# Gated mix of attention and a gated MLP: first loads on two queues, single last stores, and the last 512 rows of x turned by the load

## Chip, cores and metric

One core of one Trainium2 chip. The metric is the device time of one execution in microseconds (us). Before the change, three runs took 268.17, 269.15 and 270.21 us, median 269.15.

## What is computed

x has 2048 rows of 512 elements, bf16. Two branches start from it and are mixed row by row by a gate:

```python
x = A_x
g = _sigmoid((x * gate_w).sum(-1, keepdims=True))
# a: 32 query heads of 16, one key and one value head for all of them
q = (x @ wq) in heads;  k = x @ wk;  v = x @ wv
a = softmax(q k^T * 16**-0.5) v @ wo
# b: spatial gating MLP
z = gelu(x @ w_in)                    # 1376 = 2 * 688 columns
z1, z2 = z[..., :688], layernorm(z[..., 688:])
b = (z1 * (w_sp @ z2 + b_sp[:, None])) @ w_out
return g * a + (1 - g) * b
```

The kernel doesn't form the 2048x2048 scores. It replaces exp by a polynomial of third degree, so that the sums over all keys become moments of k and v that are computed once; a guard at the end checks that the scores were small enough, and a general path stands by if not.

## The kernel before, in words

**A planner writes the order.** The kernel describes its work as tasks (`Plan.add`, line 327), each with an engine or a choice of two, an estimated cost, what it reads and writes, and a priority (lower goes first). `Plan.run` (line 380) simulates the five engines and the DMA pipe with those estimates and so fixes each engine's program order; on the chip every engine then runs its program strictly in that order and waits on semaphores. `TUNE` (line 65) changes priority and earliest time of single tasks by their number, 25 of them before the change. DMAs of SP are issued in SP's planned order, those of ACT in ACT's. Free PSUM banks are given out by the planner too (`allowed`, line 1311); a group of products (`Group`) holds its bank until its copy out of PSUM.

**Start.** VectorE fills a tile with zeros, and TensorE runs `WARM` = 9 products of 128x512 on it (lines 843 and 844), which compute nothing. `ld_x(c)` (line 846) loads 512 rows of x, 512 KB, as they lie in memory. SP issues x's first chunk, the identity matrix `ident`, the two halves of w_in's second part (`win2`, line 851), x's second chunk, `wq` (line 857), x's third and fourth chunk, and the constants cf, cs and th (lines 860 to 862; th goes into a part of the buffer Pr). ACT issues wk, wv and gate_w (`gwl`, lines 852 to 855), then loads its table for Gelu.

**x is turned.** Nearly all products need x with its columns on the partitions (`xT`). `g_x(c)` (line 877) does this for a chunk by 16 products of 128x128 with `ident`, four to a PSUM bank, and copies the four banks to xT on ACT or VectorE (line 884). The untouched x lies in `xn`, which is the first half of the buffer of w_sp's rows (wT, line 744), so the first loads of w_sp wait for x to be read.

**After that, per chunk:** `g_kv(c)` computes k, v and the gate's sum (line 887; the copies and features follow on VectorE and POOL), `moments(c)` sums the features (line 938), and `moments_out()` makes the small matrices of the polynomial (line 948). Beside it TensorE computes the second part of z (`g_z2`, line 1121; 16 tiles, two halves, four products each) and the first two of 16 units of queries (`g_q`, line 1008; a unit is four heads for 512 rows).

**Queries go through DRAM.** The queries of a unit are stored to `qe` (line 1019) and come back spread over the partitions as Y and in part as X (`y_load`, line 1024). The load of w_in's first part (`win1`, line 1253) and the loads of w_sp are held until the first Y loads are planned. `g_z1` (line 1151) needs win1. w_sp is loaded by transposing DMAs, 128 rows to an issue, 512 KB (`ld_wT`, line 1162), each waiting for the one before; these are the only transposing loads before the change.

**Units and output.** `unit(u)` (line 1054) multiplies the third-degree form by Y: product (line 1074), then either VectorE alone (line 1083) or ACT and POOL (lines 1087, 1088). `g_sp` (line 1172) is the product with w_sp, `g_out` (line 1208) the last product, its scaling and its store. In the last 512 rows the stores go two tiles at a time, 256 KB (line 1226). Before the first of these SP waits for all other DMAs and reads the guard's flag (`finish`, line 1452).

In the profile, line 774 is the helper that records most products of 128x128 at the start, 779 and 808 those that use a part of the array; so tiles, not lines, tell these apart.

Of the kernel before, what the change touches and what calls it, by code (L numbers as in the profile page):

```python
# [34 lines left out]
WARM = 9  # L35
# [29 lines left out]
TUNE = {40: (-3, 0), 330: (0, 700), 383: (-25, 0), 403: (-3, 0), 435: (-25, 1500), 500: (-3, 0), 519: (-6, 300),  # L65
# [597 lines left out]
def build_kernel(nc, x_d, wq_d, wk_d, wv_d, wo_d, win_d, wsp_d, bsp_d, wout_d, gw_d, out_d):  # L663
    es = ExitStack()
    with es:
# [180 lines left out]
        def ld_x(c):  # L846
            load("sp", lambda q: q.dma_start(xn[:, 4 * c:4 * c + 4, :], x2[512 * c:512 * c + 512, :].rearrange("(k p) n -> p k n", p=128)), [("xn", c)], size=524288, pri=c, tag="x")
        ld_x(0)
        load("sp", lambda q: q.dma_start(ident[:], id_d), ["id"], size=32768, pri=0)
        for h in range(2):  # L850
            load("sp", lambda q, h=h: q.dma_start(win[:, :, FH + 344 * h:FH + 344 * h + 344], win_d[:, FH + 344 * h:FH + 344 * h + 344].rearrange("(dt p) n -> p dt n", p=128)), [("win2", h)], size=352256, pri=0)
# [3 lines left out]
        load("act", lambda q: q.dma_start(gwl[:], gw_d.rearrange("(one n) -> one n", one=1)), ["gwl"], size=1024, pri=-3)  # L855
        ld_x(1)
        load("sp", lambda q: q.dma_start(wq[:], wq_d.rearrange("(dt p) n -> p dt n", p=128)), ["wq"], size=524288, pri=1.5)
# [19 lines left out]
        def g_x(c):  # L877

            for dt in range(4):
                g = Group("any")  # L880
                for k in range(4):
                    add("pe", 60.0, mm1(lambda g=g: g.b, 128, 128 * k, xn[:, 4 * c + k, 128 * dt:128 * dt + 128], ident[:], True, True), r=["id", ("xn", c)], grp=g, pri=-1, tag="xT")
# [279 lines left out]
        def ld_wT(tc):  # L1162
            load("sp", lambda q: [q.dma_start(bspz[64 * i:64 * i + 1, tc % 2, :], bsp_d[512 * tc:512 * tc + 512].rearrange("(one t) -> one t", one=1)) for i in range(2)], [("bspz", tc % 2)], size=4096, n=2, pri=13, chan="bsp%d" % (tc % 2), hold=[yld[0]] if tc < 2 else [])
            for k in range(4):
                r0 = 512 * tc + 128 * k
                load("sp", lambda q, r0=r0, k=k: q.dma_start_transpose(wT[:, tc % 2, :, 128 * k:128 * k + 128], wsp_d[r0:r0 + 128, :]),
                     [("wT", tc % 2, k)] + (kfeat if tc == 1 else [("xn", c) for c in range(4)] if tc == 0 else []), size=524288, rate=DMA_TR, pri=13, chan="wT%d_%d" % (tc % 2, k), tag="wT", after=([wtl[0]] if wtl[0] else []), hold=([yld[0]] if tc < 2 else []))
                wtl[0] = pl.tasks[-1]
# [39 lines left out]
        def g_out(t2):  # L1208
# [27 lines left out]
        for c in range(4):  # L1236
            g_x(c)
# [311 lines left out]
```

## Time and profile before

| what | us |
|---|---|
| median of three runs | 269.15 |
| the profiled execution, own time | 269.58 |
| its span, first to last instruction | 267.8 |
| around the span | 1.8 |
| PE busy | 256.4 |
| DVE busy | 176.2 |
| POOL busy | 174.5 |
| ACT busy | 161.3 |

The span is what the profile's views cover; the time of a run is 1.8 us longer. PE is TensorE, PEld its weight loads (they lie beside products), DVE VectorE, POOL GpSimd, SP the engine that issues most DMAs. A matmul's length in the views contains its way through the array, so products that follow each other overlap; their spacing is the cost of one.

### The profile page before, as it was taken

To read this page: it belongs to the slowest core of one execution; us is meant where nothing else is said; L and a number is where in the kernel's file an instruction comes from. 1 tells how busy PE (TensorE), PEld (TensorE's weight loads), DVE (VectorE), ACT (ScalarE), POOL (GpSimd) and SP (SyncE) were. 2 spreads that over 40 slices of the span, in tenths; PEclk is the share of its full clock that TensorE was granted. 3 is DMA by queue.
4 is the path that set the end of the run, shared out by engine and by line. 5 is a ranking of instruction groups with operands and counts; after the bars stand their busy time and mean duration, and the time that the engine had idled before them with its cause. 6 is when DMAs were issued, how large, how long until landed. Compare 5 with 4: busy or idle time off the path is not lost. (4 is left out here: it accounts for less than half of the span.)

```text
span 267.8 us, 8031 instructions
## 1 busy us (share of the span) xinstructions
PE 256.4 (96%) x3378; PEld 124.0 (46%) x3379; DVE 176.2 (66%) x312; ACT 161.3 (60%) x209; POOL 174.5 (65%) x105
## 2 busy tenths in 40 slices
PE   7999979999999999989999989999999999999992
PEld 3686758863444433424444334434444434344450
DVE  1797969367686575784777575667687576679320
ACT  2685857789754769886476747382656563652203
POOL 8693111134697489758888989695786999998000
PEclk9999999999999999999999999999999999999998
DMA  7949975501666689969999996649697670523112
GB/s 186 350 173 245 225 93 129 81 16 53 162 214 179 143 206 184 173 175 144 217 197 222 206 251 156 189 116 226 167 184 203 147 181 14 145 85 96 39 44 84
DMA packets 54186, 42.18 MB, mean 158 GB/s; under 512 B 36249, under 2 KB 47746, under 8 KB 54146
## 3 DMA queue, kind: packets, MB, share of 16 engines
q1 hardware_dynamic: 53088, 41.59, 67.0%
q8 instruction: 27, 0.44, 0.7%
q10 hardware_dynamic: 1058, 0.03, 0.2%
q14 instruction: 13, 0.11, 0.2%
HBM read 28.51 MB, written 4.72 MB: 124 GB/s over the span
## 5 line engine op out<-in xcount | busy, mean ns | idle before, releaser
L1088 POOL TENSOR_TENSOR Pr<-Wt,Y 128x1024 bf16<-128x1024 bf16 x64 | 136.2, 2128 | 45.2 <-ACT Wt L1087 35.8
L1087 ACT ACTIVATE Wt<-ps,T1c 128x1024 bf16<-128x1024 f32 x64 | 71.3, 1114 | 53.3 <-PE ps L1074 31.7
L1083 DVE SCALAR_TENSOR_TENSOR Pr<-ps,T1c,Y 128x1024 bf16<-128x1024 f32 x64 | 81.1, 1278 | 27.1 <-PE ps L1074 26.9
L808 PE MATMUL ps<-wT,z 64*128 64x512 bf16 x598 | 92.0, 376 | 0.0
L1074 PE MATMUL ps<-X,T 64*128 64x512 bf16 x256 | 46.9, 379 | 2.1 <-ACT Wt L1087 1.2
L808 PEld LDWEIGHTS ps<-wT,z 64*128 64x128 bf16 x598 | 34.0, 94 | 31.2 <-issue 1.5
L1045 ACT ACTIVATE X<-ps 128x1024 bf16<-128x1024 f32 x32 | 31.7, 1022 | 5.5 <-PE ps L1042 5.5
L808 PE MATMUL ps<-wout,z 64*128 64x512 bf16 x169 | 30.5, 376 | 0.0
L1074 PEld LDWEIGHTS ps<-X,T 64*128 64x128 bf16 x256 | 12.0, 93 | 26.0 <-ACT Wt L1087 8.3
L808 PE MATMUL ps<-wo,win 64*128 64x512 bf16 x112 | 21.9, 377 | 0.0
L1127 ACT ACTIVATE z<-ps 128x344 bf16<-128x344 f32 x32 | 14.3, 459 | 10.0 <-PE ps L774 5.8
L779 PE MATMUL ps<-Pr,cs 128*32 128x512 bf16 x256 | 19.5, 381 | 0.0
L1192 DVE TENSOR_TENSOR z<-ps,z 128x512 bf16<-128x512 f32 x20 | 13.7, 685 | 8.2 <-PE ps L808 8.2
L1134 POOL TENSOR_TENSOR rstd<-ve,nhalf 128x4 f32<-128x4 f32 x4 | 4.3, 1080 | 20.6 <-DVE ve L1133 20.6
L1220 ACT ACTIVATE outsb<-ps,G 128x512 bf16<-128x512 f32 x10 | 6.8, 687 | 17.5 <-PE ps L808 17.1
L1116 POOL TENSOR_TENSOR win<-Ns,Rb 128x512 bf16<-128x512 f32 x12 | 15.3, 1272 | 2.4 <-POOL Pr L1088 0.7
L1129 DVE BATCH_NORM_STATS2 bst<-z 128x6 f32<-128x344 bf16 x32 | 14.5, 491 | 2.6 <-ACT z L1127 2.6
L808 PEld LDWEIGHTS ps<-wout,z 64*128 64x128 bf16 x169 | 11.1, 94 | 9.5 <-issue 0.2
L1097 DVE SCALAR_TENSOR_TENSOR Prd<-ps,T1d,Qt 128x512 bf16<-128x512 f32 x16 | 11.9, 746 | 4.3 <-PE ps L779 4.1
L779 PE MATMUL ps<-xT,win 128*32 128x512 bf16 x260 | 14.7, 379 | 0.0
L1158 ACT ACTIVATE z<-ps 128x512 bf16<-128x512 f32 x20 | 11.7, 596 | 2.9 <-PE ps L779 2.9
L774 PE MATMUL ps<-win,xT 128*128 128x344 bf16 x68 | 12.7, 309 | 0.4 <-DMA win<-in_B_w_in_dram 0.4
(148 smaller groups left out, 335.6 us busy)
## 6 DMA issues: line engine op xcount, KB each, us to landing
Y<-qe SPq DMA_DIRECT2D x32, 512.0 KB, 5.5
Rb<-rd SPq DMA_DIRECT2D x14, 256.0 KB, 5.3
wT<-in_A_x_dram SPq DMA_DIRECT2D x4, 512.0 KB, 7.9
qe<-Qt SPq DMA_DIRECT2D x64, 32.0 KB
out_dram<-outsb SPq DMA_DIRECT2D x12, 128.0 KB, 2.9
X<-qe SPq DMA_DIRECT2D x32, 32.0 KB
Pr<-c_third SPq DMA_DIRECT2D x1, 784.0 KB, 9.0
win<-in_B_w_in_dram SPq DMA_DIRECT2D x2, 344.0 KB, 5.5
```

The source lines that it names most:

```text
L774: return lambda t: t.matmul(bank(b(), n, off), lhsT, rhs, start=start, stop=stop)
L779: return [t.matmul(ps[32 * q:32 * q + 32, 512 * b() + off:512 * b() + off + n], lhsTs[q], rhss[q], start=start, stop=stop, tile_position=( ...
L808: return lambda t: t.matmul(bank(b(), n, off), lhsT[h], rhs[h], start=start, stop=stop, tile_position=(64 * z, 0))
L1045: add("act", 1030.0, lambda a, g=g, v=v: a.activation(X[:, ub, v:v + 3:2, :], bank(g.b, 1024).rearrange("p (j n) -> p j n", j=2), ACT.Square),
L1074: return [p.matmul(bank(gw.b + e), T3[64 * e:64 * e + 64, t, :], X[64 * e:64 * e + 64, ub, j, :], start=True, stop=True, tile_position=(64 ...
L1083: add("dve", 1290.0, lambda v, wv=wv, pi=pi, yv=yv, t=t: v.scalar_tensor_tensor(Pr[:, pi, :, :], wv(), T1c[:, t:t + 1], yv, ALU.add, ALU.m ...
L1087: add("act", 1040.0, lambda a, wv=wv, wi=wi, t=t: a.activation(Wt[:, wi, :, :], wv(), ACT.Identity, bias=T1c[:, t:t + 1]), r=["T1c"], w=[( ...
L1088: add("pool", 2130.0, lambda v, wi=wi, pi=pi, yv=yv: v.tensor_tensor(Pr[:, pi, :, :], Wt[:, wi, :, :], yv, ALU.mult), r=[("Y", yb, h), ("W ...
L1116: ot = lambda v, u=u, G=G: v.tensor_tensor(OT[:, tg % 2, G, :], Ns[:, u % NNS, :], rbt(G), ALU.mult)
L1127: add("act", 456.0, lambda a, g=g, h=h: a.activation(z2[:, FH * st + 344 * h:FH * st + 344 * h + 344], bank(g.b, 344), ACT.Gelu_apprx_tanh ...
L1129: add("dve", 495.0, lambda v, h=h: v.bn_stats(bst[:, st, h, :], z2[:, FH * st + 344 * h:FH * st + 344 * h + 344]), r=[("z2", st, h)], w=[( ...
L1192: add("dve", 690.0, lambda v: v.tensor_tensor(dst, bank(g.b), dst, ALU.mult), w=[("z1", ft, tc)], grp=g, evac=True, pri=3.5, tag="u")
```

## The change

- The warm-up has 7 products in place of 9.
- The first chunk of x is loaded in two halves of 256 KB. `ident`, the first half of win2 and gwl are issued by ACT, in this order and ahead of wk and wv. The second half of win2 stays on SP.
- `g_x` turns the first two 128-row tiles of a chunk for all four column blocks, then the other two, so that its four banks are open at once.
- wq's priority goes from 1.5 to 5, which places it behind x's third chunk and the new loads.
- The last 512 rows of x are not loaded to xn and not turned by products: four transposing loads of 128 rows, 128 KB each, write xT (one semaphore count for all four). They have priority 4.5 on SP's queue. `g_x(3)` is gone with its 16 products and four copies. w_sp's first loads wait only for the other three chunks.
- The last two tiles of the output are stored singly, 128 KB each; the two before them stay a pair.
- TUNE is another table, with 18 entries; task numbers have shifted.

```diff
-WARM = 9
+WARM = 7
...
-TUNE = {40: (-3, 0), 330: (0, 700), 383: (-25, 0), 403: (-3, 0), 435: (-25, 1500), 500: (-3, 0), 519: (-6, 300),
...
+TUNE = {39: (0, 1500), 316: (-12, 0), 434: (-1, 3000), 487: (-25, 0), 500: (-12, 0), 553: (6, 0), 668: (-12, 1500),
...
-        def ld_x(c):
-            load("sp", lambda q: q.dma_start(xn[:, 4 * c:4 * c + 4, :], ...), [("xn", c)], size=524288, pri=c, tag="x")
-        ld_x(0)
-        load("sp", lambda q: q.dma_start(ident[:], id_d), ["id"], size=32768, pri=0)
-        for h in range(2):
-            load("sp", ... win[:, :, FH + 344 * h:FH + 344 * h + 344] ..., [("win2", h)], size=352256, pri=0)
+        def ld_x(c, parts=1):
+            n = 4 // parts
+            for h in range(parts):
+                load("sp", lambda q, h=h: q.dma_start(xn[:, 4 * c + n * h:4 * c + n * h + n, :], ...),
+                     [("xn", c, k) for k in range(n * h, n * h + n)], size=131072 * n, pri=c, tag="x")
...
+        load("act", lambda q: q.dma_start(ident[:], id_d), ["id"], size=32768, pri=-3)
+        ld_x(0, 2)
+        ld_win2("act", 0, -3)
+        ld_win2("sp", 1, 0)
+        load("act", lambda q: q.dma_start(gwl[:], gw_d.rearrange("(one n) -> one n", one=1)), ["gwl"], size=1024, pri=-3)
...
         ld_x(1)
-        load("sp", lambda q: q.dma_start(wq[:], ...), ["wq"], size=524288, pri=1.5)
-        for c in range(2, 4):
-            ld_x(c)
+        load("sp", lambda q: q.dma_start(wq[:], ...), ["wq"], size=524288, pri=5)
+        ld_x(2)
...
+        load("sp", lambda q: [q.dma_start_transpose(xT[:, :, 1536 + 128 * k:1664 + 128 * k], x2[1536 + 128 * k:1664 + 128 * k, :]) for k in range(4)], [("x", 3, dt) for dt in range(4)], size=524288, n=4, pri=4.5, rate=DMA_TR, tag="xT")
...
         def g_x(c):
 
+            gr = [Group("any") for _ in range(4)]
+            for k0 in (0, 2):
+                for dt in range(4):
+                    g = gr[dt]
+                    for k in (k0, k0 + 1):
+                        add("pe", 60.0, mm1(...), r=["id", ("xn", c, k)], grp=g, pri=-1, tag="xT")
             for dt in range(4):
-                g = Group("any")
-                for k in range(4):
-                    add("pe", 60.0, mm1(...), r=["id", ("xn", c)], grp=g, pri=-1, tag="xT")
+                g = gr[dt]
...
             if not last:
...
+            elif k > 1:
+                tail.append(load("sp", lambda q: q.dma_start(out2[128 * t2:128 * t2 + 128, :], outsb[:, k, :]), [("out", t2)], r=[("ob", k)], size=131072, pri=0, chan="o%d" % k, tag="out"))
             elif k % 2:
...
         for c in range(4):
-            g_x(c)
+            if c < 3:
+                g_x(c)
             g_kv(c)
             moments(c)
```

## Rows read from the trace of the kernel before

**Rows 1.** The page's busy times: engine, busy us, share of the span, instructions.

```profile
PE 256.4 (96%) x3378; PEld 124.0 (46%) x3379; DVE 176.2 (66%) x312; ACT 161.3 (60%) x209; POOL 174.5 (65%) x105
```

**Rows 2.** Stretches: length, then PE, PEld, DVE, ACT, POOL busy, clock, DMA share, GB/s.

```profile
0.00:5.87 5.87, 4.12 (x10) 1.28 (x11) 0.70 (x4) 1.49 (x2) 4.88 (x13) 1.00 0.67 167
5.87:12.00 6.13, 5.69 (x71) 4.15 (x72) 4.01 (x16) 3.77 (x8) 3.71 (x6) 1.00 1.08 347
...
100.00:263.00 163.00, 160.43 (x1911) 66.99 (x1909) 107.12 (x125) 91.79 (x100) 121.88 (x63) 1.00 0.70 155
263.00:267.80 4.80, 0.00 (x0) 0.00 (x0) 0.00 (x0) 0.69 (x1) 0.00 (x0) 0.72 0.34 116
```

**Rows 3.** PE in order of time: start, length, what, count, idle before and releaser.

```profile
1.19 4.02 PE L844 MATMUL ps<-Pr 128*128 128x512 bf16 x9 [1.19 <-DVE Pr L840]
...
4.57 0.63 PE L844 MATMUL ps<-Pr 128*128 128x512 bf16 x1
5.77 0.17 PE L774 MATMUL ps<-ones,gwl 1*128 1x1 bf16 x1 [0.56 <-DMA gwl<-in_gate_w_dram]
5.87 1.07 PE L774 MATMUL ps<-ident,wT 128*128 128x128 bf16 x16
...
7.03 0.90 PE L774 MATMUL ps<-win,xT 128*128 128x344 bf16 x5
...
8.32 0.61 PE L774 MATMUL ps<-win,xT 128*128 128x344 bf16 x3 [0.39 <-DMA win<-in_B_w_in_dram]
...
18.24 0.48 PE L774 MATMUL ps<-wkvg,xT 128*128 128x33 bf16 x13
...
36.69 4.26 PE L779 MATMUL ps<-win,xT 128*32 128x344 bf16 x110 [1.84 <-issue]
```

**Rows 4.** The turns by form, to 60 us: count | busy us, mean ns | idle.

```profile
L774 PE MATMUL ps<-ident,wT 128*128 128x128 bf16 x64 | 5.0, 219 | 0.0
```

**Rows 5.** First issue of x; landings of x (first chunk), ident and win2 (line 851).

```profile
0.73 0.43 SPq L847 DMA_DIRECT2D wT<-in_A_x_dram  x1
...
wT<-in_A_x_dram SPq DMA_DIRECT2D x1, 512.0 KB, 4.2
ident<-c_id SPq DMA_DIRECT2D x1, 32.0 KB, 4.2
DMA to landing us min/median/max: 5.0/5.5/6.0
```

**Rows 6.** wq and win1: issues and landings, first z1 products; w_sp's transposing loads.

```profile
3.34 0.52 SPq L857 DMA_DIRECT2D wq<-in_A_wq_dram  x1
wq<-in_A_wq_dram SPq DMA_DIRECT2D x1, 512.0 KB, 7.9
22.79 0.59 SPq L1253 DMA_DIRECT2D win<-in_B_w_in_dram  x1
win<-in_B_w_in_dram SPq DMA_DIRECT2D x1, 688.0 KB, 10.4
40.65 13.26 PE L779 MATMUL ps<-xT,win 128*32 128x512 bf16 x240
L1166 SPq DMA_TRANSPOSE wT<-in_B_w_sp_dram x16: 1772/3303/8607, 24.3 to 192.9; - x16
36.70:41.80 5.10, 5.10 (x132) 4.28 (x135) 3.82 (x14) 3.20 (x7) 0.00 (x0) 1.00 0.76 113
```

**Rows 7.** The end: last copy; stores issued in 263:268, 254:256.5 and 248:250, us to landing.

```profile
263.09 0.69 ACT L1220 ACTIVATE outsb<-ps,G 128x512 bf16<-128x512 f32 x1 [0.30 <-PE ps L779]
...
out_dram<-outsb SPq DMA_DIRECT2D x1, 256.0 KB, 3.5
...
out_dram<-outsb SPq DMA_DIRECT2D x2, 128.0 KB, 2.9
...
out_dram<-outsb SPq DMA_DIRECT2D x2, 128.0 KB, 1.8
```

More of the change, by code (lines that the diff above doesn't have):

```diff
@@ L845, in build_kernel, with ld_win2 @@
         add("dve", 100.0, lambda v: v.tensor_copy(qk1[:, 7:8], bank(gw_.b, 1)), w=["junk"], grp=gw_, evac=True, pri=0)
-        def ld_x(c):
-            load("sp", lambda q: q.dma_start(xn[:, 4 * c:4 * c + 4, :], x2[512 * c:512 * c + 512, :].rearrange("(k p) n -> p k n", p=128)), [("xn", c)], size=524288, pri=c, tag="x")
-        ld_x(0)
-        load("sp", lambda q: q.dma_start(ident[:], id_d), ["id"], size=32768, pri=0)
-        for h in range(2):
-            load("sp", lambda q, h=h: q.dma_start(win[:, :, FH + 344 * h:FH + 344 * h + 344], win_d[:, FH + 344 * h:FH + 344 * h + 344].rearrange("(dt p) n -> p dt n", p=128)), [("win2", h)], size=352256, pri=0)
+        def ld_x(c, parts=1):
+            n = 4 // parts
+            for h in range(parts):
+                load("sp", lambda q, h=h: q.dma_start(xn[:, 4 * c + n * h:4 * c + n * h + n, :], x2[512 * c + 128 * n * h:512 * c + 128 * n * (h + 1), :].rearrange("(k p) n -> p k n", p=128)),
+                     [("xn", c, k) for k in range(n * h, n * h + n)], size=131072 * n, pri=c, tag="x")
+        def ld_win2(eng, h, pri):
+            load(eng, lambda q: q.dma_start(win[:, :, FH + 344 * h:FH + 344 * h + 344], win_d[:, FH + 344 * h:FH + 344 * h + 344].rearrange("(dt p) n -> p dt n", p=128)), [("win2", h)], size=352256, pri=pri)
+        load("act", lambda q: q.dma_start(ident[:], id_d), ["id"], size=32768, pri=-3)
[3 more added lines that the diff above has]
+        load("act", lambda q: q.dma_start(gwl[:], gw_d.rearrange("(one n) -> one n", one=1)), ["gwl"], size=1024, pri=-3)
         load("act", lambda q: q.dma_start(wkvg[:, :, 0:16], wk_d.rearrange("(dt p) d -> p dt d", p=128)), ["wk"], size=16384, pri=-3)
@@ L854, in build_kernel @@
         load("act", lambda q: q.dma_start(wkvg[:, :, 16:32], wv_d.rearrange("(dt p) d -> p dt d", p=128)), ["wv"], size=16384, pri=-3)
-        load("act", lambda q: q.dma_start(gwl[:], gw_d.rearrange("(one n) -> one n", one=1)), ["gwl"], size=1024, pri=-3)
         ld_x(1)
-        load("sp", lambda q: q.dma_start(wq[:], wq_d.rearrange("(dt p) n -> p dt n", p=128)), ["wq"], size=524288, pri=1.5)
-        for c in range(2, 4):
-            ld_x(c)
+        load("sp", lambda q: q.dma_start(wq[:], wq_d.rearrange("(dt p) n -> p dt n", p=128)), ["wq"], size=524288, pri=5)
+        ld_x(2)
         load("sp", lambda q: q.dma_start(cf[:], cf_d), ["cf"], size=8704, pri=5)
@@ L877, in g_x @@
         def g_x(c):
+            gr = [Group("any") for _ in range(4)]
[3 more added lines that the diff above has]
+                    for k in (k0, k0 + 1):
+                        add("pe", 60.0, mm1(lambda g=g: g.b, 128, 128 * k, xn[:, 4 * c + k, 128 * dt:128 * dt + 128], ident[:], True, True), r=["id", ("xn", c, k)], grp=g, pri=-1, tag="xT")
             for dt in range(4):
-                g = Group("any")
-                for k in range(4):
-                    add("pe", 60.0, mm1(lambda g=g: g.b, 128, 128 * k, xn[:, 4 * c + k, 128 * dt:128 * dt + 128], ident[:], True, True), r=["id", ("xn", c)], grp=g, pri=-1, tag="xT")
+                g = gr[dt]
                 dst = xT[:, dt, 512 * c:512 * c + 512]
@@ L1166, in ld_wT @@
                 load("sp", lambda q, r0=r0, k=k: q.dma_start_transpose(wT[:, tc % 2, :, 128 * k:128 * k + 128], wsp_d[r0:r0 + 128, :]),
-                     [("wT", tc % 2, k)] + (kfeat if tc == 1 else [("xn", c) for c in range(4)] if tc == 0 else []), size=524288, rate=DMA_TR, pri=13, chan="wT%d_%d" % (tc % 2, k), tag="wT", after=([wtl[0]] if wtl[0] else []), hold=([yld[0]] if tc < 2 else []))
+                     [("wT", tc % 2, k)] + (kfeat if tc == 1 else [("xn", c, k) for c in range(3) for k in range(4)] if tc == 0 else []), size=524288, rate=DMA_TR, pri=13, chan="wT%d_%d" % (tc % 2, k), tag="wT", after=([wtl[0]] if wtl[0] else []), hold=([yld[0]] if tc < 2 else []))
                 wtl[0] = pl.tasks[-1]
```

2 lines of the change are left out of this document (added), and 3 rows, old and new, of the table TUNE.

## Prediction

> **What bounds the kernel now.** I read the page's busy times first, then the busy time by stretch, then the start and the end in order of time, and last the DMA issues. The first view names the engine: TensorE (PE) is busy for 256.4 of 267.8 us, the next engine for about two thirds [rows 1]. The stretches say where its other 11.4 us lie [rows 2]: 1.75 us before 5.87, 0.44 up to 12, 2.57 in all of 100 to 263, and 4.80 after 263, where the last results are scaled and stored. The order in time shows one more, of 1.84 us ahead of 36.69 [rows 3]. Stalls of ACT, DVE or POOL in between cost nothing, since PE always has another product. So the time is made of four things: when useful products begin, how much PE has to do, what it waits, and what follows its last product. 4.0 of its busy us are the nine warm-up products, which compute nothing; those of 128x512 start (4.57 - 1.19)/8 = 0.42 us apart, 512 columns at 1.2 GHz, and the 16 turns that begin at 5.87 are (1.07 - 0.22)/15 = 0.057 us apart, 128 columns at 2.4 GHz (0.22 is the last one's own length) [rows 3, 4]. The granted-clock column reads 1.00 before 5.87 as well; the spacing shows the lower level there.
>
> **The change, part by part.**
>
> *The start.* PE is free at 4.57 + 0.63 = 5.20 and waits until 5.77, by the profile for gwl, the third load on ACT's queue [rows 3]. The first 512 rows of x, issued first on SP at 0.73, had landed at 4.9, and ident, issued behind them, half a microsecond later [rows 5]. After the change ident is first on ACT's queue, so by its 4.2 us [rows 5] it lands at about 4.9; the first half of x lands no later than the whole did; seven warm-up products end near 1.19 + 6 x 0.42 + 0.63 = 4.4. The first eight turns can start at 5.0 in place of 5.87. At the lower clock they are 0.107 us apart, so they take until 5.9. The second half (issued at about 1.2, plus 4.2) is there by then, and its eight turns end at 6.3 to 6.7, against 6.94 before. The first z2 product came at 7.03, and PE then stood for 0.39 us at 8.32 for the second half of win2 [rows 3]. Each half of win2 moves up one place in a queue, about 0.5 us by the issue time in rows 6 (they landed 5.0 and 6.0 us after their issue) [rows 5]. I take 0.35 us for the earlier z2 and 0.35 for the gap: 0.7 us. Bounds: 0, if gwl still stands ahead of the turns in PE's program or win2 lands no earlier because the 16 DMA engines are shared (they move 347 GB/s from 5.87 on) [rows 2], and 1.3 (5.87 - 5.0, plus the 0.44 idle before 12). What lies beside it: ACT issues five loads where it issued three, so its table load comes about 1 us later, beside the turns and ahead of the first copy out of PSUM, which must wait for them; wk and wv come later too, but kv stands behind the first z2 products. With the four banks of a chunk turned side by side, the first copy waits for some nine more turns (0.5 us); in chunks 1 and 2 z2 products cover that, without them it costs 0.5 each.
>
> *The 16 turns of the last 512 rows.* The 64 turns keep PE busy for 5.0 us [rows 4], so a quarter is 1.26; by their spacing 16 take 0.9; in a row they took 1.07 [rows 3]. I take 1.0. Four copies out of PSUM go too, from ACT and DVE, which do not set the end: nothing.
>
> *The loads that come instead.* Four transposing loads stand in SP's queue, and wq, cf, cs and th now come behind them and behind x's third chunk. wq was issued at 3.34 and landed at 11.24 [rows 6]. The third chunk adds 512 KB at 347 GB/s, 1.5 us. The nearest rows for the four are the 512 KB transposing loads of w_sp: one alone in its stretch kept the DMA engines busy for 0.76 x 5.1 = 3.9 us [rows 6]. At the speed of plain loads it would be 1.5. So wq lands at 14.2 to 16.6, most likely near 16, and xT's last chunk 1.5 us before it, at 12.7 to 15.1. Everything behind wq shifts by 3 to 5.4 us: Q, its way through DRAM, Y, then win1. win1 was issued at 22.79 and landed at 33.2, and the first product that needs it started at 40.65 [rows 6]: 7.4 us of cover, 5.6 with PE some 1.8 earlier. So wq may land as late as 16.9 for nothing. cs and th shift too, but the products that read them first need Q or the moments of all chunks as well. While Q waits, PE has z2 of the first three chunks, 96 products at up to 0.18 us each (five in 0.90 us) [rows 3], some 15 us. Cost 0; without the cover each us of lateness is one of time.
>
> A rule speaks to this. The Trainium skill's "Advanced Engine Details and Errata", section "X-Bar Transpose (TRN2)", says that transposing loads are as fast as plain ones on this chip, 350 to 400 GB/s expected. The 113 GB/s in the stretch of rows 6 do not agree. By the rule (an estimate from that page) the four would take 1.5 us, and the slow case among the rivals would not exist; by the row the sum is the same, and that case stays.
>
> *The end.* The last copy out of PSUM runs from 263.09 to 263.78, and the 256 KB store behind it lands 3.5 us after its issue [rows 7]. After the change the third tile's 128 KB go ahead while PE still works on the fourth, and the last store is 128 KB. Stores of that size close by landed after 1.8 and 2.9 us. I take 2.8, because that pair followed each other as the last two will: 0.7 us less, between 0.5 and 1.7.
>
> *The order of the work.* TUNE has 18 entries for 25, so the planner orders the middle anew. The products themselves stay. The gaps it can touch are the 2.57 us of 100 to 263 and the 1.84 ahead of 36.69; the latter is put down to "issue", that is to nothing visible [rows 2, 3]. I take 0, between -4 and +3.
>
> *Sum.* 0.7 + 1.0 + 0.7 = 2.4 us. The profiled execution took 269.58 (span 267.8, 1.8 around it): 267.2. The median of the runs shown is 0.43 lower, so 266.8 against 269.15. The small bounds of the parts (0, 0.9, 0.5) give 267.8, the large ones (1.3, 1.26, 1.7) 264.9. About one per cent, 2.7 us, is what a measurement of this kernel can tell from no change: faster means below 266.5.
>
> **Rivals.**
>
> 1. *The gap ahead of 36.69 goes too.* It lies in the stretch in which the first w_sp transposing load and win1 fill the DMA engines; with these 3 to 5 us later and PE earlier, it may fall away. Against it: nothing shows its cause. 266.8 - 1.8 = 265.0.
>
> 2. *The clock rises later.* With two warm-up products fewer, PE stands for 0.6 us from 4.4. It stood for 0.57 before and had the higher level at 5.87, which speaks against it. If the rise waited as long from the first turn as it did from the first warm-up product (5.87 - 1.19 = 4.7 us, so to 9.7), work between would run at half speed: about 1.9 us lost, 268.7. The Trainium skill's "TensorE: Matmul & The Clock Gate", section "What's actually happening", has activity as what lifts the lower level, which is the default; the spacing in rows 3 agrees with that order of events, and by the rule fewer warm-up products are a risk.
>
> 3. *The transposing loads hold SP, and the last chunk is late.* 16 loads of this kind held SP for 1.8 to 8.6 us, median 3.3, at four times the bytes [rows 6]. Should each of the four hold it for 3.3 regardless of size, SP is busy from 3.9 (where wq's issue ended before, and x's third chunk was next) to 17.1, and the last lands 4.2 later, at 21.3. PE's order has kv of the last chunk where it stood at 18.24 [rows 3], some 2.7 us earlier now: 15.5. From a landing later than that PE stands, for 5.8 us here: 272.6, slower than before. Against it: a quarter of the bytes and few loads ahead in the queue.
>
> 4. *The change does not do what it says, or the new order takes it back.* The start is set by win2 anyway and gaps in the middle double: 0.7 less gain and about 2 us more waiting, 269.4.
>
> **How the numbers follow.** Forecast 0.45, with its own range of 264.9 to 267.8, about half of it below 266.5. Rival 1: 0.15; rival 2: 0.12; rival 3: 0.10; rival 4: 0.18. Faster by over 1%: 0.23 + 0.15 = 0.38. Slower by over 1% (above 271.8): rival 3, 0.10. The rest, 0.52, is within 1%. The range of 264.2 to 270.0 takes in the forecast and rivals 1, 2 and 4 and leaves rival 3 and the tails out.
>
> **What would show it.** Right: first turns near 5.0 and z2 before 6.8; 48 turns in place of 64 and PE busy for 1 us less, plus some 0.9 for two warm-up products; wq landing at 14 to 17 with no wait of PE for a DMA between 12 and 41; the last store landing within 3 us. Wrong: a wait of PE for xT or win1, turns or z2 at twice their spacing after 6, or more than 5 us of idle PE between 12 and 263.

## The result, and the profile after

Twenty executions of the kernel after have a median of 270.07 us (269.54 to 271.12), twenty of the kernel before beside them 268.54 (266.42 to 270.74): a ratio of 1.005, with a 95% interval of 1.003 to 1.0069. The change costs half a per cent, 1.5 us. That is inside the one per cent that was called "no change", but the forecast was 266.8 (0.991 of the 269.15 before), the sign is the other one, and 270.07 lies just beyond the range that ended at 270.0. Ratios and intervals, here and below, leave out single executions in a slower state; the medians and ranges keep them.

The profiled execution took 269.99 us, its span is 268.1. The page's busy times, which answer to [rows 1]:

```profile
PE 258.8 (97%) x3309; PEld 119.4 (45%) x3309; DVE 173.2 (65%) x307; ACT 161.8 (60%) x209; POOL 176.0 (66%) x106
```

PE is busy for 2.4 us more than before, although two warm-up products (0.8 us) and 16 turns (about 1.0) are gone. It idles 9.3 us in place of 11.4. The stretches say where, and answer to [rows 2]; the columns are the same:

```profile
0.00:5.87 5.87, 4.57 (x21) 2.30 (x22) 0.57 (x3) 1.63 (x3) 4.88 (x13) 1.00 0.60 191
5.87:12.00 6.13, 4.39 (x25) 2.12 (x23) 2.07 (x5) 1.75 (x4) 1.74 (x4) 1.00 1.24 276
12.00:34.00 22.00, 21.35 (x274) 15.29 (x272) 19.40 (x78) 13.95 (x28) 13.13 (x10) 1.00 0.61 174
34.00:37.00 3.00, 3.00 (x54) 1.86 (x55) 2.55 (x15) 2.04 (x4) 0.00 (x0) 1.00 1.08 240
...
100.00:263.00 163.00, 161.81 (x1949) 68.16 (x1947) 106.92 (x126) 98.24 (x109) 128.48 (x66) 1.00 0.75 162
263.00:268.10 5.10, 0.67 (x6) 0.09 (x1) 0.75 (x1) 0.69 (x1) 0.00 (x0) 0.85 0.29 97
```

Idle before 5.87 fell from 1.75 to 1.30. From 5.87 to 12 it rose from 0.44 to 1.74, and PE finished 25 products there, where it had finished 71. The gap of 1.84 us ahead of 36.69 is gone (34 to 37 is full), and 100 to 263 lost 1.4 us of idle time. So later stretches gain, and the first twelve microseconds lose more. In order of time PE shows this, answering to [rows 3]:

```profile
1.19 3.17 PE L843 MATMUL ps<-Pr 128*128 128x512 bf16 x7 [1.19 <-DVE Pr L839]
4.47 1.86 PE L773 MATMUL ps<-ident,wT 128*128 128x128 bf16 x16
7.36 1.04 PE L773 MATMUL ps<-win,xT 128*128 128x344 bf16 x3 [1.03 <-DMA win<-in_B_w_in_dram]
...
10.48 1.04 PE L773 MATMUL ps<-win,xT 128*128 128x344 bf16 x3 [0.71 <-DVE xT L894]
11.31 1.91 PE L773 MATMUL ps<-ident,wT 128*128 128x128 bf16 x16
13.02 0.66 PE L773 MATMUL ps<-wkvg,xT 128*128 128x33 bf16 x16
...
13.76 0.73 PE L773 MATMUL ps<-ident,wT 128*128 128x128 bf16 x8
```

The turns begin 1.4 us earlier than before, at 4.47, but 16 of them take 1.86 us: (1.86 - 0.22)/15 = 0.11 us apart, 128 columns at 1.2 GHz. The second chunk's turns at 11.31 still have that spacing (1.91 for 16); the eight at 13.76 are the first with half of it. The clock column reads 1.00 all along, so only the spacing shows the level. Before, the higher level was there at 5.87. From 4.47 to 13.98 PE is busy for 1.40 + 4.39 + 1.98 us (to 5.87, to 12 and to 13.98), 7.77 in all (the expectation below has 7.65), at half speed: up to 3.9 us lost.

Two waits stand in the same rows: 1.03 us for win2 ahead of 7.36, and 0.71 for a copy of xT by VectorE ahead of 10.48. Why that copy came late stands in VectorE's own order:

```profile
5.94 0.69 DVE L894 CAST xT<-ps 128x512 bf16<-128x512 f32 x1 [1.39 <-PE ps L773]
9.64 0.18 DVE L860 TENSOR_SCALAR wkvg<-wkvg 128x64 bf16<-128x64 bf16 x1 [3.01 <-DMA wkvg<-in_A_wk_dram]
9.73 0.69 DVE L894 CAST xT<-ps 128x512 bf16<-128x512 f32 x1
```

VectorE copies one block of the first chunk, then is to scale wk (line 860), waits 3.01 us for that load, and only then copies the last block, whose products were ready by 6.33. The landings, answering to [rows 5] and [rows 6] (size, us from issue to landing):

```profile
win<-in_B_w_in_dram ACTq DMA_DIRECT2D x1, 344.0 KB, 5.1
win<-in_B_w_in_dram SPq DMA_DIRECT2D x1, 344.0 KB, 5.6
...
ident<-c_id ACTq DMA_DIRECT2D x1, 32.0 KB, 2.9
...
wkvg<-in_A_wk_dram ACTq DMA_DIRECT2D x1, 16.0 KB, 7.2
```

and SP's issues:

```profile
1.73 0.47 SPq L852 DMA_DIRECT2D win<-in_B_w_in_dram  x1
2.24 1.21 SPq L848 DMA_DIRECT2D wT<-in_A_x_dram  x2
3.49 7.32 SPq L868 DMA_TRANSPOSE xT<-in_A_x_dram  x4
10.86 0.58 SPq L863 DMA_DIRECT2D wq<-in_A_wq_dram  x1
```

wk is issued by ACT at 2.42, behind ident, half of win2 and gwl, and lands 7.2 us later, at 9.6. ACT's half of win2 lands at 1.18 + 5.1 = 6.3, SP's at 1.73 + 5.6 = 7.33, and the new TUNE (task 316, moved by -12) puts a z2 product that reads SP's half first. The four transposing loads hold SP for 7.32 us, wq is issued at 10.86 and lands at 15.7. At the end, answering to [rows 7]:

```profile
263.33 0.69 ACT L1230 ACTIVATE outsb<-ps,G 128x512 bf16<-128x512 f32 x1 [1.68 <-PE ps L807]
263.77 0.75 DVE L1231 TENSOR_SCALAR outsb<-ps,G 128x512 bf16<-128x512 f32 x1 [2.04 <-PE ps L807]
264.55 1.19 SPq L1236 DMA_DIRECT2D out_dram<-outsb  x2
```

Both last copies run side by side. From the end of the later one (264.52) to the end of the span it is 3.6 us; before it was 4.0.

### The profile page after: what moved, and what is told of

Read it like the earlier page. It is cut to its first block, busy times and chain, and to the rows that moved or that the text cites. A ratio compares the mean times of both kernels' runs of the same rounds, so it can differ in the third digit from the quotient of the medians.

```text
span 268.1 us, 7889 instructions
## 1 busy us (share of the span) xinstructions
PE 258.8 (97%) x3309; PEld 119.4 (45%) x3309; DVE 173.2 (65%) x307; ACT 161.8 (60%) x209; POOL 176.0 (66%) x106
## 5 line engine op out<-in xcount | busy, mean ns | idle before, releaser
L807 PE MATMUL ps<-wT,z 64*128 64x512 bf16 x600 | 93.8, 376 | 0.0
L807 PEld LDWEIGHTS ps<-wT,z 64*128 64x128 bf16 x600 | 35.3, 94 | 33.3 <-issue 0.5
L1084 PE MATMUL ps<-X,T 64*128 64x512 bf16 x256 | 46.0, 380 | 1.0 <-ACT Wt L1097 0.6
L807 PE MATMUL ps<-wout,z 64*128 64x512 bf16 x159 | 34.3, 376 | 0.0
L807 PE MATMUL ps<-wo,win 64*128 64x512 bf16 x120 | 26.1, 376 | 0.0
L773 PE MATMUL ps<-win,xT 128*128 128x344 bf16 x88 | 17.1, 328 | 2.4 <-DMA win<-in_B_w_in_dram 1.0
L778 PE MATMUL ps<-Pr,cs 128*32 128x512 bf16 x256 | 19.4, 381 | 0.0
L807 PEld LDWEIGHTS ps<-wout,z 64*128 64x128 bf16 x159 | 11.8, 94 | 8.6 <-DVE z L1202 0.2
L778 PE MATMUL ps<-xT,win 128*32 128x512 bf16 x272 | 15.6, 379 | 0.0
L1106 ACT ACTIVATE Ns<-ps,S 128x512 f32<-128x512 f32 x12 | 8.2, 686 | 12.0 <-PE ps L778 11.8
```

Of the source, the lines that this page charges most:

```text
L773: return lambda t: t.matmul(bank(b(), n, off), lhsT, rhs, start=start, stop=stop)
L778: return [t.matmul(ps[32 * q:32 * q + 32, 512 * b() + off:512 * b() + off + n], lhsTs[q], rhss[q], start=start, stop=stop, tile_position=( ...
L807: return lambda t: t.matmul(bank(b(), n, off), lhsT[h], rhs[h], start=start, stop=stop, tile_position=(64 * z, 0))
L1084: return [p.matmul(bank(gw.b + e), T3[64 * e:64 * e + 64, t, :], X[64 * e:64 * e + 64, ub, j, :], start=True, stop=True, tile_position=(64 ...
```

## The experiments

The planner's programs lie in `pg.ops`, one list for each engine. Most edits move or replace single operations there after planning, so that everything else keeps its order. Each ratio is to executions of the kernel before on the same chip; it is not the quotient of the medians given. A profile shows one execution, a ratio all of them.

### Is it the warm-up or the gaps?

Four runs: the kernel after with nine warm-up products, with wk's load second on ACT's queue, with both; and the kernel before with its last two warm-up products cut to one column.

```diff
 after, a_w9: the last warm-up task issues three products
-        for _ in range(WARM):
-            add("pe", 430.0, lambda t: t.matmul(bank(gw_.b), ...), ...)
+        for i in range(WARM):
+            add("pe", 430.0, lambda t, i=i: [t.matmul(bank(gw_.b), ...) for _ in range(3 if i == WARM - 1 else 1)], ...)
 after, a_wk (a_w9_wk: both)
         res = pl.run(pg, allowed)
+        ld = pg.ops["act"]
+        ld.remove(wk_op)
+        ld.insert(1, wk_op)
 before, b_w7: the last two with one column
+            ... t.matmul(bank(gw_.b, 512 if i < WARM - 2 else 1), Pr[:, 0, 0, 0:128], Pr[:, 0, 0, 0:512 if i < WARM - 2 else 1], ...)
```

Nine warm-up products. 

> The changed kernel with nine warm-up products in place of seven, every engine's order otherwise unchanged. Theory W (the shorter warm-up is what keeps TensorE at the lower clock): turns and the first z2 products, 0.107 and 0.287 us apart in the changed kernel until 13.98, are at 0.057 and 0.15 from about 6 on; of the 7.65 us that PE was busy between 4.47 and 13.98 about 3 go, time 1.1% below the changed kernel's, near 267. Theory G (the gaps behind the turns, waits for win2 and for a copy, keep it there): the spacing stays at the lower level until about 14, time unchanged within 0.3%.

Measured: 269.42 (267.88 to 270.0), ratio 1.0038 (0.9999 to 1.0076). In its profile most of the turns (16 in 1.29 us) and the first z2 products run at the higher level, and then it is lost. The turns, then the stretches 5.87 to 12 and 12 to 14, columns as in [rows 2]:

```profile
4.57 1.29 PE L773 MATMUL ps<-ident,wT 128*128 128x128 bf16 x16
...
5.87:12.00 6.13, 3.05 (x24) 2.08 (x25) 1.88 (x5) 1.60 (x5) 1.74 (x4) 0.91 1.25 270
12.00:14.00 2.00, 2.00 (x32) 1.86 (x30) 1.29 (x2) 1.18 (x2) 0.00 (x0) 0.50 0.92 225
```

PE is busy for 3.05 of 6.13 us, waiting 1.5 for win2 and 1.5 for the copy of xT; then the granted clock is 0.50. So the higher level, once there, is lost behind the gaps. That it was the nine products that brought it is not shown: by its ratio the run is not told apart from the kernel after, and in single profiles the first 16 turns took 1.07 to 1.83 us with nine products (the kernel before and a_best are the ends) and 1.28 to 1.91 with seven (a_wk and a_dve).

wk's load second. 

> The changed kernel with wk's load second on ACT's queue in place of fourth. In the changed kernel VectorE stands for 3.01 us until wk lands at 9.6, with the last copy of the first chunk's xT behind it, and PE waits 0.71 us for that copy. Theory G (gaps at the start keep the lower clock): the wait goes and the clock rises by about 8 to 10, so 2 to 3 us less, 267 to 268. Theory W (the warm-up alone decides): only the wait goes and the second half of z2 moves up, 0.7 to 1.2 us less, the spacing of the products stays doubled until 14.

Measured: 270.16 (267.35 to 270.82), 1.0052 (1.001 to 1.0094). wk came early, and win2 late: PE waited for win2 twice, until 7.29 and again until 9.37, and the granted clock was 0.50 from 12 to 14.

```profile
4.48 1.28 PE L773 MATMUL ps<-ident,wT 128*128 128x128 bf16 x16
7.29 0.32 PE L773 MATMUL ps<-win,xT 128*128 128x344 bf16 x1 [1.53 <-DMA win<-in_B_w_in_dram]
9.37 0.75 PE L773 MATMUL ps<-win,xT 128*128 128x344 bf16 x2 [1.77 <-DMA win<-in_B_w_in_dram]
```

The product at 7.29, with seven warm-up products, has the length of the higher level (0.32; 0.47 at the lower), and behind the second wait the level is lost. A load of 16 KB put ahead of ACT's half of win2 pushed that half from 6.3 to 9.4.

Both. 

> Both of the two edits before. Theory W: as with nine warm-up products, and the wait of 0.71 us as well, about 4 us less than the changed kernel, 266. Theory G: as with wk alone. If either edit is enough for the clock, this has the time of the better one less the wait.

Measured: 268.38 (267.81 to 270.9), 1.0038 (1.0004 to 1.0072), with 2.4 us of waits for win2 and the same fall. Neither is a cure.

Seven in the kernel before. 

> The kernel before with its last two warm-up products cut to one column, every order unchanged. Theory W: the clock rises several us later than 5.7; of the 7.7 us of PE work up to 14 about 2 to 3 us are lost, 270 to 271.5 against 268.5. Theory G: dense turns and z2 products follow at 5.87 as before, the clock rises with them, time the same within 0.3%.

Measured: 269.28 (266.91 to 270.14), 1.0062 (1.0028 to 1.0095). Nothing but the warm-up is changed there, and PE's order shows turns and z2 at half speed:

```profile
5.72 0.18 PE L774 MATMUL ps<-ones,gwl 1*128 1x1 bf16 x1 [1.34 <-DMA gwl<-in_gate_w_dram]
5.83 1.89 PE L774 MATMUL ps<-ident,wT 128*128 128x128 bf16 x16
...
7.82 2.48 PE L774 MATMUL ps<-win,xT 128*128 128x344 bf16 x8
10.09 0.61 PE L774 MATMUL ps<-wkvg,xT 128*128 128x33 bf16 x16
```

In the kernel before the 16 turns took 1.07 and the eight z2 products 1.5 us [rows 3]. Two warm-up products fewer cost 1.7 us by the medians (269.28 against 267.57), in a start with nothing else changed. That is the price of rival 2 in the order of before, measured. PE stands longer ahead of the turns with it (1.34 us in place of 0.56), so the shorter warm-up and the longer gap are not told apart.

### The parts alone, on the kernel before

First loads on two queues. The edit issues ident, win2, gwl, wk and wv on ACT in that order, x's first chunk in two halves, and puts the scaling of wk behind two copies of VectorE; PE's order is that of before, with nine warm-up products.

```diff
         res = pl.run(pg, allowed)
+        for o in (idl, w2):
+            sp.remove(o)
+            o.eng = "act"
+        ac[0:3] = [idl, w2, gw_l, wk_, wv_]
+        x0.fn = lambda q: [q.dma_start(xn[:, 2 * h:2 * h + 2, :], ...) for h in range(2)]
```

> The kernel before with the change's first loads alone: x's first chunk in two halves, ident, the first half of win2 and gwl on ACT's queue ahead of wk and wv (VectorE's scaling of wk placed behind its two copies of the first chunk). Nine warm-up products and all other orders as before. The prediction's term: turns from 5.0 to 5.8, z2 from about 6.7, 0.7 us less. Rival (the queue order costs more than it gives): wk, behind the 344 KB of win2, lands near 9.6 in place of 5.2, kv's first products, 8.77 before, wait for it, and PE stands for about 1 us: 0 to 1 us more, and more where the gap brings the lower clock.

Measured: 272.83 (270.46 to 275.0), 1.0136 (1.0091 to 1.0181). This is far more than the change as a whole costs:

```profile
5.54 1.07 PE L774 MATMUL ps<-ident,wT 128*128 128x128 bf16 x16
...
7.74 2.47 PE L774 MATMUL ps<-win,xT 128*128 128x344 bf16 x8 [0.97 <-DMA win<-in_B_w_in_dram]
11.61 0.61 PE L774 MATMUL ps<-wkvg,xT 128*128 128x33 bf16 x16 [1.40 <-DMA wkvg<-in_A_wv_dram]
```

The turns begin 0.33 us earlier, but z2 begins 0.7 us later, behind win2, kv (at 8.8 in the kernel before) waits for wv, and the clock falls between the turns and z2. In the old order of PE the new loads are simply late; in the kernel after kv comes at 13.02, behind wv's landing at 11.3, so that wait doesn't show there.

Transposing loads for the last 512 rows. They stand where x's fourth chunk was issued; the 16 turns and four copies go.

```diff
+        x3.op.fn = lambda q: [q.dma_start_transpose(xT[:, :, 1536 + 128 * k:1664 + 128 * k], x2[1536 + 128 * k:1664 + 128 * k, :]) for k in range(4)]
+        pg.ops[e] = [o for o in pg.ops[e] if o not in gone]
```

> The kernel before with the last 512 rows of x loaded by four transposing loads in the place of the plain load in SP's queue (so behind wq), without their 16 turns and four copies; every other order as before. The prediction's term: 1.0 us less PE work and no wait, since kv of that chunk stood at 18.24: about 1 us less. Rival: SP is held for about 7 us in place of 1.6, cf, cs and th land some 5 us later, and products of 25 to 28 wait: no gain, or up to 2 us more.

Measured: 274.01 (271.67 to 274.83), 1.0197 (1.0159 to 1.0235). SP is held from 5.10 to 12.40, so qe's first stores come at 15.16, the Y loads at 22.31 (18.88 before) and win1 at 27.27 (22.79). No wait for the last chunk or for win1 shows. What shows is a gap of 2.08 us with no releaser ahead of 36.58, and behind it the clock:

```profile
34.00:37.00 3.00, 0.92 (x26) 0.46 (x18) 2.52 (x8) 0.73 (x2) 1.01 (x1) 1.00 1.21 204
37.00:46.00 9.00, 9.00 (x172) 7.21 (x164) 8.80 (x32) 5.38 (x11) 2.30 (x2) 0.81 0.60 137
```

Against the profiled execution of the kernel before (269.58) this one, 271.67, is 2.1 us longer. By the rows (1 - 0.81) x 9.00 = 1.7 us of that lie in the lower clock, 0.24 in the gap, which was 1.84 before, and 0.9 in longer waits for Wt (2.1 us in place of 1.2); the missing turns give some 0.9 back. The execution was also the fastest of its five; of the 2.3 us from it to the median no profile exists.

Single last stores. 

> The kernel before with the last pair of output tiles stored singly; all else as before. The prediction's term: the last landing 0.7 us earlier (0.5 to 1.7). From the changed kernel, where the two stores were issued 0.39 us apart behind one another: 0.4 less. Rival (the stores' fixed cost): no change.

```diff
+        for t2 in (14, 15):
+            o = Op("sp", lambda q, t2=t2: q.dma_start(out2[128 * t2:128 * t2 + 128, :], outsb[:, t2 % 4, :]), ...)
```

Measured: 268.24 (266.39 to 270.74), 0.9982 (0.9956 to 1.0008): 0.5 us less, not told apart from nothing.

### The start mended

Three steps on the kernel after: VectorE scales wk behind its last copy of the first chunk (a_dve); that with nine warm-up products and the last two stores in the order of their copies (a_fix); that with the halves of win2 exchanged between ACT and SP (a_best).

```diff
 a_dve
+        dv[i_], dv[i_ + 1] = dv[i_ + 1], dv[i_]
 a_fix, also
+        sp[-2], sp[-1] = sp[-1], sp[-2]
 a_best, also
+        ac[ia], sp[ib] = h1, h0
+        h1.eng, h0.eng = "act", "sp"
```

> The changed kernel with nine warm-up products, VectorE's scaling of wk behind the last copy of the first chunk in place of ahead of it, and the last two stores issued in the other order (the tile that ACT finishes first goes first). Theory S (the loss is the start: sparse products there and the lower clock that follows): the wait of 0.7 to 1.5 us for the copy goes, PE between 5.9 and 12 is busy for over 4.5 of 6.1 us, the clock's fall at 11 is rarer, and the end is 0.4 shorter: 1.5 to 2.5 us below the changed kernel, 267.5 to 268.5. Theory M (the loss is in the middle, by the new order): only the 0.4 of the end, 269.5.

Measured: 267.78 (267.32 to 268.7), 0.9989 (0.9967 to 1.0011). The clock does not fall in its profile, and PE is busy for 4.28 us of 5.87 to 12 (over 4.5 expected), with the higher level.

> The kernel after with one change: VectorE scales wk behind its last copy of the first chunk to xT, not ahead of it; still 7 warm-up products, and the end as it is. If VectorE's order is a cause of its own, the wait of 0.7 us at 10.48 goes and PE's products of the first chunk close up, so that the spacing halves some 1 to 2 us earlier than at about 14: about 1.2 us less than the kernel after, a ratio to before of about 1.001. If the two missing warm-up products alone decide, products go on at the lower clock to about 14 and the ratio stays at 1.005. If only both together help, as the run with 9 products alone (1.0038) suggests, it lies at 1.003 to 1.004.

Measured: 268.03 (267.68 to 269.12), 0.9993 (0.9964 to 1.0021). One exchange of neighbours on VectorE takes 1.5 us off the kernel after; its ten executions all lie below the twenty of the kernel after. With seven warm-up products:

```profile
4.14 1.91 PE L773 MATMUL ps<-ident,wT 128*128 128x128 bf16 x16
7.39 0.61 PE L773 MATMUL ps<-win,xT 128*128 128x344 bf16 x3 [1.33 <-DMA win<-in_B_w_in_dram]
...
10.00 0.84 PE L773 MATMUL ps<-ident,wT 128*128 128x128 bf16 x12 [0.40 <-DVE wkvg L1246]
11.35 0.57 PE L773 MATMUL ps<-wkvg,xT 128*128 128x33 bf16 x16 [0.51 <-DMA wkvg<-in_A_wv_dram]
```

The turns are still slow, but z2 at 7.39 is not ((0.61 - 0.31)/2 = 0.15 us apart, 344 columns at 2.4 GHz; in the kernel after (1.04 - 0.47)/2 = 0.29 from 7.36, 0.47 being the length of one at 8.49), and the level holds; the wait for the copy of xT is gone. PE is busy for 256.5 us in all, 2.3 less than in the kernel after with the same products. One thing this profile does not settle: the level had risen by 7.39, ahead of the exchanged operations. That the exchange decides is shown by the executions (10 against 20, no overlap; the intervals of the two ratios don't meet), not by the path in one of them. Behind the exchange the warm-up shows no price: seven products here and nine in a_fix have the same ratio within their intervals. The nine-product run fits: with VectorE's old order its ten executions spread from 267.9 to 270.0.

> The kernel after with all mended: 9 warm-up products, VectorE's scaling of wk behind the copies, the last two stores in the order of their copies, and the two halves of win2 exchanged, so that ACT, whose load landed at 6.1, brings the half that PE reads first, and SP, whose load landed at 7.1, the other. The first copies of xT end at about 6.6, so the first z2 product should come at 6.6 to 6.8 in place of 7.16: 0.3 to 0.5 us less than the same kernel without the exchange (ratio 0.9989), a ratio of about 0.997, 267.2 at 268.0 before. If PE then only waits for the second half instead, or for wk and wv as before, the ratio stays at 0.999.

Measured: 267.66 (267.21 to 268.76), 0.9978 (0.9952 to 1.0005). The first z2 product comes at 7.05 (6.6 to 6.8 expected), and what it waits for is now a copy (0.22 us), not win2; PE is busy for 4.92 us of 5.87 to 12. With z2 early, kv now waits for wv:

```profile
11.40 0.57 PE L773 MATMUL ps<-wkvg,xT 128*128 128x33 bf16 x16 [0.83 <-DMA wkvg<-in_A_wv_dram]
```

Its interval lies wholly below that of the kernel after. It has the lowest ratio of the three, not told apart from the other two; beside the kernel before, 0.6 us less is not told apart from nothing.

### The gap with no releaser

[rows 3] had a gap of 1.84 us ahead of 36.69 put down to "issue". It was gone in the kernel after and there in the run with the transposing x loads. First the load that stands beside it was moved: SP's first transposing load of w_sp behind the loads of X.

```diff
+        sp.insert(last, sp.pop(i_))
```

> The kernel before with one change: SP issues the first transposing load of w_sp behind the two loads of X, not ahead of them. In the kernel before PE stood for 1.84 us at 34.85 to 36.69 with no releaser shown, and went on when that load's successor was issued (36.74). If the transposing load and what follows it on the queues is the cause, the gap goes or moves with it, PE goes on at 34.85, and the time falls by up to 1.8 us (ratio 0.993 to 0.997). If the gap belongs to PE's own program at that place (its long run of 128x32 products), it stays with 1.5 to 2 us at the same instruction and the ratio is 1.000, or more if later loads of w_sp come too late.

Measured: 267.65 (266.06 to 268.82), 0.9977 (0.9945 to 1.0009), not told apart from no change. The gap went:

```profile
29.64 8.93 PE L779 MATMUL ps<-win,xT 128*32 128x344 bf16 x240
```

The same move with the transposing x loads and the single stores:

> The kernel before with three parts, its order kept: the last 512 rows of x by transposing loads, single last stores, and SP's first transposing load of w_sp behind the loads of X. The transposing x loads alone gave a ratio of 1.0197, with PE standing for 2.1 us at 34.5 to 36.6, the lower clock from about 37.7 to 41, and Y and win1 3.4 to 4.5 us later; the moved load alone gave 0.9977 and the stores 0.9982. If the loss of the transposing x loads came by that gap and the clock behind it, both are gone here, the 16 turns are 0.9 us less work, and the ratio is 0.99 to 0.995 (266 to 267). If it came from the later Y, win1 and w_sp, which stay late here, the ratio stays at 1.010 to 1.016 with waits of PE for Wt or w_sp after 40.

Measured: 268.46 (267.81 to 273.06), 1.0038 (1.0004 to 1.0072). Of the two per cent that the transposing x loads cost alone, 1.6 are gone, and the granted clock from 37 to 46 is 1.00 in place of 0.81; but the gap itself stayed, with 2.21 us, so moving the load is not the whole of it. PE in order of time, of this run, then of the run with the transposing x loads alone:

```profile
28.89 5.57 PE L779 MATMUL ps<-win,xT 128*32 128x344 bf16 x146
36.68 3.54 PE L779 MATMUL ps<-win,xT 128*32 128x344 bf16 x92 [2.21 <-issue]
```

```profile
28.92 5.57 PE L779 MATMUL ps<-win,xT 128*32 128x344 bf16 x146
36.58 3.73 PE L779 MATMUL ps<-win,xT 128*32 128x344 bf16 x64 [2.08 <-issue]
```

Both stop after 146 of the 240 quarter products of z2; the kernel before stopped after 130, and it had 16 turns more. 146 + 48 = 130 + 64: the same count of PE's instructions, not the same work. So a run with 32 more one-column products at the start, which compute nothing:

```diff
+            ... [t.matmul(bank(gw_.b, 512 if j == 0 else 1), ...) for j in range(33 if i == WARM - 1 else 1)]
```

> The kernel before with 32 more warm-up products of one column each behind the ninth, which compute nothing. In the kernel before and in the two runs with the transposing x loads that show the gap, PE stood still after 473 or 474 recorded products, though 16 turns were missing from two of them: at the same count of PE's instructions, not at the same work. If PE runs out of program there, the gap comes after some 474 products again, 32 of the z2 products earlier (about 98 of the 240 quarter products before it, not 130), and a packet of the instruction queue starts 2 to 3 us before PE goes on. If the gap belongs to the work or to the transposing load, it stays behind about 130 quarter products.

Measured, in one execution: 268.62.

```profile
29.47 3.82 PE L779 MATMUL ps<-win,xT 128*32 128x344 bf16 x98
33.75 5.43 PE L779 MATMUL ps<-win,xT 128*32 128x344 bf16 x142 [0.46 <-issue]
```

98 products, as forecast: 98 + 64 + 32 = 194 again. PE stops at a place in its program. What comes for it there shows in the DMA queues, where a queue of kind "instruction" moves packets of 16 KB (columns: packets, MB, share of 16 engines' time; a packet counts where it starts). In the kernel before, 33.8 to 34.0:

```profile
q8 instruction: 1, 0.02, 30.8%
```

With the first w_sp load moved, 31.4 to 31.6, and with 32 products more, 31.3 to 31.5:

```profile
q8 instruction: 1, 0.02, 32.7%
```

```profile
q8 instruction: 1, 0.02, 32.3%
```

A packet takes 0.308 x 16 x 0.2 = 1.0 us. In the kernel before it starts at 33.8 to 34.0 and PE goes on at 36.69; in the run with 32 products more at 31.3 to 31.5 with PE on at 33.75, in both cases 2.2 to 2.9 us later. With the load moved the packet starts 2.4 us earlier than before; 2.5 us later it is 34.0, and PE, at 29.64 + 130 x 0.037 = 34.5 in front of the same product, does not stop. So PE ran out of program, and a late packet is the gap. That this queue is PE's is inferred: it moves 27 packets in the kernel before, one for some 250 of PE's 6757 products and weight loads.

Three runs above agree. b_tail, b_w7 and b_start have PE's order of before, and PE stops behind the same 130 products, but for 0.74, 0.79 and 1.27 us; the packets start at 32.8 to 33.0, 34.4 to 34.6 and 37.6 to 37.8, and PE goes on at 35.24, 37.02 and 40.18, 2.2 to 2.6 us later. In b_tail:

```profile
29.51 4.99 PE L779 MATMUL ps<-win,xT 128*32 128x344 bf16 x130
35.24 4.26 PE L779 MATMUL ps<-win,xT 128*32 128x344 bf16 x110 [0.74 <-issue]
```

So the place belongs to the program, and the length changes from run to run with the packet's time; 1.84 is that of one execution. What made the packet late is not shown; the load that b_gap moves is among those in flight ahead of it. The Trainium skill's "Runtime: NRT & Kernel Launch", section "Instruction fetch mechanics", says that an engine fetches its program ahead in 16 KiB blocks over a DMA queue of its own, and that the cost is mostly hidden. The size agrees with these packets; "mostly" leaves room for this place, where it cost 0.46 to 2.21 us.

The moved load with the single stores:

> The kernel before with two parts: SP's first transposing load of w_sp behind the loads of X (alone 0.9977), and the last two tiles stored singly (alone 0.9982). The two lie at different ends and should add: 0.996, 267.0 at 268.0 before, with an interval that leaves 1 out. If the moved load's gain was chance, it is 0.998 and the interval holds 1.

Measured: 267.21 (265.84 to 268.97), 0.9978 (0.9943 to 1.0013). The parts did not add beyond what a measurement tells, and neither the version of the kernel before nor a_best is shown to beat it.

## Why the prediction was wrong, point by point

**The start (-0.7): wrong, and it is the cause of the loss.** The forecast let the turns begin at 5.0 and z2 before 6.8. The turns came at 4.47, earlier even, but z2 at 7.36. Each half of win2 did move up, to 6.3 and 7.3; the step that failed is "0.35 us for the earlier z2", which took the order of PE's first z2 products as it was. The new order begins with the later half (a_best, which exchanges the two, starts z2 at 7.05). Beside it stands the sentence that wk and wv come later "but kv stands behind the first z2 products". It looked at PE's order alone. On VectorE the scaling of wk stands ahead of a copy that z2 needs, and wk's landing at 9.6 held z2 through VectorE for 0.71 us. "Stalls of ACT, DVE or POOL in between cost nothing" does not hold there: the prediction had not looked at VectorE's order in the first 12 us, and that single pair of operations is worth 1.5 us (a_dve against the kernel after). On PE's own order the sentence on kv fails too as soon as z2 is early: kv then waits for wv, for 0.51 to 0.83 us (a_dve, a_fix, a_best).

**Rival 2: right in the order of before, taken at 0.12; in the new order it is not the whole.** Its argument against itself, that PE had stood for 0.57 us before as well and had the higher level at 5.87, fell with b_w7: with two warm-up products fewer, turns and z2 run at half speed up to about 10 and 1.7 us are lost, where the rival had reckoned 9.7 and 1.9. In the kernel after the rise comes at about 14, with the waits for win2 and xT in between, and the 7.77 us of work at the lower level are up to 3.9 lost. There nine products alone bring nothing that can be told from chance (1.0038 against 1.005), and behind the exchange on VectorE seven do as well as nine. That the clock falls again where it had risen, behind thin work, is shown by a_w9, and was in no part of the forecast.

**The 16 turns (-1.0): right, and covered over.** 48 turns remain, and no product waits for the transposed chunk. Counted from each product's start to the next one's, idle time left out, the turns take 2.78 us in b_x3_gap, which keeps the order and the warm-up of before, in place of 3.67: 0.9 less. In the kernel after the 48 take 4.58, the clock's doing. By the same count z2 takes 20.9 us in place of 19.4, again the clock, and the products that are neither warm-up, turns, z2, kv nor gate 228.1 in place of 227.5, which is the order; so PE is busier in spite of fewer products.

**The loads (0): right for the change, wrong as a reason.** wq landed at 15.7 (14.2 to 16.6 forecast), and no load was waited for between 12 and 41. SP was held for 7.3 us, 1.8 for each of the four; rival 3's 3.3 did not come. But the same loads in the old order cost 2% (b_x3); its profile puts 1.7 us of that to the lower clock behind the gap, and 1.6% come back when the w_sp load and the stores are changed too. win1 was issued 4.5 us later, inside the forecast 3 to 5.4, landed at 35.2 and was first needed at 37.75, so the cover was enough; the planner's new order, which knew of the loads, may have a share in that.

**The end (-0.7): mis-sized.** The last stores land 2.7 us after their issue, within the forecast, yet the tail fell by 0.4 us (4.0 to 3.6): the copies of the last two tiles run side by side, so SP issues both stores behind the later one, 0.4 us apart. In the order of before, where one copy follows the other, the tail is 3.2 us in b_tail's profile (the last copy ends at 261.87, the span at 265.1), 0.8 less, as the prediction had it; over all executions b_tail's ratio gives 0.5 us, not told apart from nothing.

**The order (0): between.** The gap ahead of 36.69 went, as rival 1 had it, and PE's waits for Wt and X fell from 2.0 to 1.0 us. Against that, "the products themselves stay" was wrong in one respect: the planner also chooses how a group of products is cut. 88 z2 products run whole and 160 as quarters, before 68 and 240. For z2 this costs nothing: by the count above whole ones and quarters together take 19.4 us in the kernel before and in a_fix. But the other products take 0.6 us more in the new order, in a_fix as in the kernel after; which of them, and by what, is not shown. A wait of 0.65 us for Q is new. The gap's worth outside the profiled execution is less than its 1.84: b_gap, without it, is 0.6 us faster (from 1.5 faster to 0.2 slower).

**What stays open.** With the start mended (a_best) the kernel is 0.6 us faster than before, not 2.35. In its profile the start costs 0.5 us where 0.7 was to be gained: the 0.39 for win2 is gone, but z2 comes at 7.05 against 7.03, and kv waits 0.83. The turns give 1.0 where the clock allows it, the tail 0.5 (3.5 in place of 4.0), the waits for Wt and X and the gap 1.6; the order's 0.6 and Q's 0.65 go off. By that a_best should be about 1.4 us faster, and its interval reaches from 1.3 faster to 0.1 slower; what lies between has no name here.

## What to carry to other kernels

When loads at the start are put on other queues, walk through every engine's order up to the first dense work, not only that of the engine that bounds: a small operation that waits for a late load stalls whatever stands behind it on its engine. A gap in the first microseconds can cost more than its length: here the clock was granted late (at about 14 us in the kernel after), or taken back (a_w9), behind thin work; the spacing of one form of product at two places shows it. And a wait put down to "issue" can be tested by a count: if the stop moves with the number of instructions ahead of it, the engine is out of program, and the instruction packets in the DMA queues say when more came.

## What the runs showed of the hardware that was not expected

- The clock fell again within the first 11 us after it had risen, with PE busy for 3.05 of 6.13 us (a_w9), and once in the middle, behind a gap of 2.08 us (b_x3, granted clock 0.81 from 37 to 46). The gaps of 1.84 us in the kernel before and of 2.21 in b_x3_gap left the clock at 1.00 in their profiles.
- A 16 KB load issued second on ACT's queue made the 344 KB load behind it land about 3 us later (a_wk); behind that load it took 7.2 us itself.
- Four transposing loads of 128 KB held SP for 7.32 us, 1.8 each on the mean, and wq behind them landed 4.8 us after its issue (7.9 in the kernel before). By the rule weighed in the prediction, from the Trainium skill's "Advanced Engine Details and Errata", section "X-Bar Transpose (TRN2)", transposing loads are as fast as plain ones; 512 KB issued over 7.32 us, 72 GB/s, does not agree, though here the issue sets the pace and other loads share the DMA engines.
- A late packet of PE's program stopped it for 0.46 to 2.21 us at a fixed count of instructions, in seven profiled executions (the kernel before, b_tail, b_w7, b_start, b_x3, b_x3_gap, b_count).
